# Four loads of an opening moved to later places in their queues: w_out's second half, two quarters of w_in, and the last slice of Bs

## The chip, the core and the metric

The kernel runs on one NeuronCore of a Trainium2 chip. A core has TensorE (PE, matmuls), VectorE (DVE), ScalarE (ACT), GpSimd (POOL) and SyncE (SP), each with its own instruction queue that is worked off in order, and 16 DMA engines that move data between the chip's memory (HBM) and the core's on-chip memory (SBUF). DMAs are issued by SP (here the profile's queue q1) and by POOL (q0); an issue is an instruction in that engine's queue. The metric is the device time of the whole kernel in microseconds (us). Before the change three runs gave 921.84, 922.67 and 922.73 us, median 922.67 us.

## The reference

Inputs are x (8 x 3008 x 256), two 256 x 256 matrices w_r and w_i with biases, and an expert layer w_in (256 x 2048) and w_out (2048 x 256), all float32.

```python
X = np.fft.rfft(x, axis=1)                        # per batch, along the 3008 positions
Yr = Xr @ w_r - Xi @ w_i + b_r
Yi = Xr @ w_i + Xi @ w_r + b_i
Y  = softshrink(Yr, 0.01) + 1j * softshrink(Yi, 0.01)
y  = np.fft.irfft(Y, n=3008, axis=1)              # back to 8 x 3008 x 256
h  = y.reshape(24064, 256) @ w_in
g  = np.where(h > 0, h, np.exp(np.minimum(h, 0)) - 1)      # ELU
out = g @ w_out                                   # 24064 x 256
```

## The kernel before

**Stages.** A batch's Fourier transform of length 3008 = 47 x 64 is done in stages of matmuls, with two passes through DRAM to reorder. For a batch b they are: A (six units: x times the 64-point table M1, written to DRAM as DA), Z (DA read back in another order, in two reads: slots 0 to 7, then slots 8 to 31), X (eight units on Z, giving XT), M (twelve units: XT times the weights, bias, softshrink, giving Y), B (six units on Y, written to DRAM as DB), Bs (DB read back in four slices, 0 to 3), and Y (eight units, two on each slice of Bs, giving yT). Then the expert layer takes yT in blocks of 512 tokens, and for each block in 8 steps: `front` (four matmuls of yT with w_in_s, and Exp), `elu` and `finish_elu` (DVE, sometimes POOL), and two steps later `back` (eight matmuls with w_out_r). Step i uses columns 256 (i mod 8) to 256 (i mod 8) + 255 of w_in: a quarter q of w_in, 512 columns, serves two steps, so quarter 2 is first used by front(4), quarter 3 by front(6). The second half of w_out is first used by back(4), which stands behind front(6).

**Order of the work.** Everything is written out by hand, and each engine's queue holds its instructions in the order of the program. An opening does all of batch 0 up to Bs, and stage A of batch 1, without expert work beside them. After it a loop over i runs the 376 steps of the expert layer, and a plan puts units of the next batches between its steps: f0[t] ahead of front(t), f1[t] behind `finish_elu`. For batch 0 the plan has Y(0,2) ahead of front(1), Y(0,3) to Y(0,5) ahead of front(2) to front(4), X(1,0) ahead of front(5), X(1,1) ahead of front(6), X(1,2) ahead of front(7), and Y(0,6), the first unit on slice 3 of Bs, ahead of front(21). In f1[3] a `gate` (a POOL copy of one column, which holds up POOL's queue until a tile has landed) waits for Z(1)'s second read, and then POOL issues the loads of x for batch 2 (in f1[3], f1[8] and f1[13]).

**Loads in the opening.** w_in comes in four quarters of 512 KB on SP's queue (`load_w_in`, L564), each into a staging tile, from where `scale_w_in` multiplies it by 2/S into the bf16 tile w_in_s (L641 on DVE for quarters 0 to 2, L643 on ACT for quarter 3). The order on SP's queue is: w_in(0); DB write 0; w_in(1); DB write 1; w_in(2); DB write 2; w_in(3); DB writes 3, 4, 5; Bs slices 0 and 1; DA write 0; Bs 2; DA write 1; Bs 3; DA write 2; the two reads of Z(1); then the output's writes. On POOL's queue: a gate on Z(0); the three loads of x for batch 1; w_out's two halves of 1 MB (`load_w_out`, L569); the softshrinks of `first_M` (L224, L225); the two halves of the table M4 (L632); the gate on Z(1) and the loads of x for batch 2; then the M units of batch 1 (L204, L205).

Between stages of the opening, `idle_pe(n)` (L292) puts n matmuls on a constant tile, whose result nobody reads.

Of the kernel before, what the change touches and what calls it, by code (L numbers as in the profile page):

```python
# [8 lines left out]
ALU = mybir.AluOpType  # L9
AF = mybir.ActivationFunctionType  # L10
# [19 lines left out]
def kernel(  # L30
# [11 lines left out]
    nc = tc.nc  # L42
    P = nc.NUM_PARTITIONS

    B, S, D = x.shape
# [59 lines left out]
    Bs_of = {}  # L105
# [22 lines left out]
    def unit_A(b, u, alone=False, on_dve=False, ahead=False):  # L128
        ci, uu = u // 2, u % 2
        if uu == 0:  # L130
            if ahead and ci > 0:
                A_of[b, ci] = late3.tile([P, 8, D], BF16, name="A", tag="gT")
            elif alone:
                A_of[b, ci] = wk4.tile([P, 8, D], BF16, name="A", tag="Bs")
            else:
                A_of[b, ci] = wk2.tile([P, 8, D], BF16, name="A", tag="A")
            if ci == 0:
                DA_of[b] = dram.tile([NJ, P, D], BF16, name="DA", tag="DA")
        xt, A = xts[ci], A_of[b, ci]
        dav = DA_of[b].rearrange("j p d -> p j d")  # L140
        ps = unit_ps("aps", alone or ahead)
        for j in range(2):
            nc.tensor.matmul(  # L143
                ps[:, j, :], lhsT=M1[:],
                rhs=xt[:, 4 * uu + 2 * j : 4 * uu + 2 * j + 2, :], start=True, stop=True,
            )
        evac(
            A[:, 4 * uu : 4 * uu + 4, :].rearrange("p n d -> p (n d)"),
            ps[:].rearrange("p a b -> p (a b)"), on_dve,
        )  # L150
        j0 = 8 * ci
        if alone:
            j0 += 4 * uu
            nc.sync.dma_start(dav[:, j0 : j0 + 4, :], A[:, 4 * uu : 4 * uu + 4, :])
        elif uu == 1:
            nc.sync.dma_start(dav[:, j0 : j0 + 8, :], A[:])

    def load_Z(b, s0, s1):

        if b not in Z_of:  # L160
            Z_of[b] = zp.tile([2 * NR, NS, D], BF16, name="Z", tag="Z")
        dv = DA_of[b].rearrange("j (h c s) d -> (j h c) s d", h=2, c=2)
        nc.sync.dma_start(Z_of[b][:, s0:s1, :], dv[:, s0:s1, :])
# [50 lines left out]
    def first_M(q, i, eng):  # L214

        ps = pre1.tile([P, 2 * D], F32, name="mps1", tag="mps1")
        yb, clip = m_group(0, q, i, ps[:])
        let_go()
        Y_ = Y_of[0, q][:, i, :]
        if eng is nc.scalar:  # L220
            nc.scalar.activation(clip[:], yb[:], AF.Relu, bias=lam_n[:])
            held.append((Y_, yb, clip))
        else:
            eng.tensor_scalar(clip[:], yb[:], LAM, -LAM, ALU.min, ALU.max)  # L224
            eng.tensor_tensor(Y_, yb[:], clip[:], ALU.subtract)  # L225
# [35 lines left out]
    def load_Bs(b, w):  # L261

        Bs = wk4.tile([4 * K1, 8, D], BF16, name="Bs", tag="Bs")
        dv = DB_of[b].rearrange("k (c h m) d -> (k c h) m d", c=2, h=2)
        nc.sync.dma_start(Bs[:], dv[:, 8 * w : 8 * w + 8, :])
        Bs_of[b, w] = Bs
# [22 lines left out]
    def idle_pe(n):  # L289

        for _ in range(n):
            nc.tensor.matmul(ips[:], lhsT=busy[:, 0:P], rhs=busy[:], start=True, stop=True)  # L292
# [264 lines left out]
    w_in_f = []  # L557

    def load_w_in(q):
        if q < 3:  # L560
            wf = late3.tile([P, 2, FQ], F32, name="w_in_f", tag="Et")
        else:
            wf = late2.tile([P, 2, FQ], F32, name="w_in_f", tag="osb")
        nc.sync.dma_start(wf[:], w_in_v[:, :, q * FQ : q * FQ + FQ])  # L564
        w_in_f.append(wf)

    def load_w_out(hh):
        hf = slice(hh * NFT // 2, (hh + 1) * NFT // 2)
        nc.gpsimd.dma_start(w_out_r[:, hf, :], w_out_v[:, hf, :])  # L569

    def gate(src):

        t = gatep.tile([P, 1], F32, name="gate", tag="gate")
        nc.gpsimd.tensor_copy(t[0 : src.shape[0], :], src)


    def fB(v, on_dve=False):
        unit_B(0, v, alone=True, on_dve=on_dve)
# [3 lines left out]
    for ci in range(3):  # L582
        load_x(1, ci)
    load_w_out(0)
    load_w_out(1)
    for u in range(8):
        unit_X(0, u, alone=True, on_dve=u in (1, 4, 7))
        if u == 1:
# [25 lines left out]
    first_M(2, 1, nc.scalar)  # L614
    first_M(3, 0, nc.gpsimd)
    fB(1)
    load_w_in(2)
    first_M(3, 1, nc.scalar)
    first_M(4, 0, nc.gpsimd)
    fB(2)  # L620
    load_w_in(3)
    first_M(4, 1, nc.scalar)
    first_M(5, 0, nc.scalar)
    fB(3)
# [6 lines left out]
    for h, w in enumerate((w40, w41)):  # L631
        nc.gpsimd.tensor_scalar(  # L632
            M4v[:, :, h], r4[0 : 2 * NR], w[0 : 2 * NR], None, ALU.mult
        )
    load_Bs(0, 0)
    load_Bs(0, 1)

    def scale_w_in(q, on_dve):
        dst = w_in_s[:, :, q * FQ : q * FQ + FQ]
        if on_dve:  # L640
            nc.vector.tensor_scalar_mul(dst, w_in_f[q][:], 2.0 / S)  # L641
        else:
            nc.scalar.activation(dst, w_in_f[q][:], AF.Copy, scale=2.0 / S)  # L643


    scale_w_in(0, True)
    for u in range(6):
        unit_A(1, u, on_dve=bool(u % 2), ahead=True)
        if u in (1, 3):
            scale_w_in((u + 1) // 2, True)  # L650
            load_Bs(0, 2 + u // 2)
        idle_pe(2)
    scale_w_in(3, False)
    for s0, s1 in ((0, 8), (8, NS)):
        load_Z(1, s0, s1)
    idle_pe(3)
    for u in range(2):
        unit_Y(0, u, alone=True, on_dve=bool(u % 2))
# [117 lines left out]
    def put(kind, b, *a):  # L776
        return ({"A": unit_A, "X": unit_X, "M": unit_M, "B": unit_B, "Y": unit_Y}[kind], (b, *a))

    def plan(b):

        f0 = [[] for _ in range(PER)]
        f1 = [[] for _ in range(PER)]
        n1, n2 = b + 1, b + 2
        mid = [("X", u) for u in range(8)] + [
            ("M", 0, 0), ("M", 0, 1), ("M", 1, 0), ("M", 1, 1), ("B", 0), ("M", 2, 0),
            ("M", 2, 1), ("B", 1), ("M", 3, 0), ("M", 3, 1), ("B", 2), ("M", 4, 0),
            ("M", 4, 1), ("B", 3), ("M", 5, 0), ("M", 5, 1), ("B", 4),
            ("A", 0), ("B", 5), ("A", 1), ("A", 2), ("A", 3), ("A", 4),
        ]
        if n1 < B:  # L790
            lead, seq = int(b == 0), [("y", u) for u in range(2, 6)] + mid
            seq.insert(20, ("y", 6))
            seq.insert(24, ("y", 7))
            xs = (3, 8, 13)
            seq += [("A", 5), ("n", 0), ("n", 1)] if b else [("n", 0), ("n", 1), ("A", 5)]
        else:
            lead, seq = 0, [("y", u) for u in range(2, 8)]
        for t, u in enumerate(seq, lead):
            if u[0] == "y":
                f0[t].append(put("Y", b, u[1]))  # L800
            elif u[0] == "n":
                f0[t].append(put("Y", n1, u[1]))
            elif u[0] == "A":
                if n2 < B:
                    f0[t].append(put("A", n2, u[1]))
            else:
                f0[t].append(put(u[0], n1, *u[1:]))
            if u == ("A", 1):
                f1[t] += [(load_Bs, (n1, w)) for w in range(4)]
            if u == ("A", 5) and n2 < B:  # L810
                f1[t] += [(load_Z, (n2, s0, s1)) for s0, s1 in ((0, 8), (8, NS))]
        if b == 0:
            f1[xs[0]].append((lambda: gate(Z_of[1][:, 16, 0:1]), ()))
        if n2 < B:
            for ci in range(3):
                f1[xs[ci]].append((load_x, (n2, ci)))
        return f0, f1
# [3 lines left out]
    for i in range(n + LAG):  # L821
        if i < n:
            r = i % PER
            if r == 0:
                f0, f1 = plan(i // PER)
                used = [bool(u0 or u1) for u0, u1 in zip(f0, f1)]
            free = not used[r]
            bare = bare + 1 if free else 0
            calm = free and (i >= n - 2 or (r + 2 < PER and not used[r + 1] and not used[r + 2]))
            for f, a in f0[r]:  # L830
                f(*a)
            on_act = any(f is unit_M for f, a in f0[r])
            h = front(i, calm and bare % 3 == 2, on_act)
        finish_elu()
        if i < n:
            for f, a in f1[r]:
                f(*a)
            split = not free and i > LAG and (i - LAG) % NPAIR == NPAIR - 1
            if split:
                back(i - LAG, True)  # L840
            elu(i, *h, free and i > 0, on_act)
        else:
            split = False
        if i >= LAG and not split:
            back(i - LAG, False)
# [30 lines left out]
```

## Time and profile before

| What | Value |
|---|---|
| median of three runs | 922.67 us |
| the profiled execution, its own time | 922.12 us |
| its span | 920.3 us |
| PE busy | 897.0 us, 97% of the span |
| DVE busy | 753.4 us, 82% |
| ACT busy | 695.0 us, 76% |
| POOL busy | 263.3 us, 29% |
| SP's queue (q1) | 77.61 MB |
| POOL's queue (q0) | 27.26 MB |

The profile's times are microseconds from the start of the span. A line of the timeline gives start, duration, engine, line of the kernel, operation, output and inputs, number of instructions and, in brackets, how long the engine sat idle before it and what ended that. SPq and POOL rows with DMA_DIRECT2D are the issues of transfers; the transfer itself runs later. "DMA Z<-DA" in the chain is the time from an issue to the landing of its last byte. PE's busy time includes the filler matmuls. The granted clock is 1.00 when TensorE runs at full speed.

### The profile page before, as it was taken

The page shows a single profiled execution, that of the slowest core. Times are in us where ns is not written, and L with a number is a line of the kernel's source. Part 1 is how long each engine was busy: PE and PEld are TensorE (multiplying, and loading weights), DVE is VectorE, ACT ScalarE, POOL GpSimd, SP SyncE. Part 2 cuts the span into 40 slices and gives each one's busy share as a digit, 9 for nine tenths or more (in the row PEclk, how much of TensorE's full clock was granted, in tenths as well). Part 3 has the DMA queues.
Part 4 walks back from the last instruction along what each step waited for, and adds up shares of the span by engine and source line. Part 5 has one row for each costly group of instructions (what it writes and reads, how often), then busy time and mean ns, then how long its engine had stood idle before and what let it go on. Part 6 is the DMA issues. An engine that isn't in the chain of part 4 may idle for free.

```text
span 920.3 us, 17019 instructions
## 1 busy us (share of the span) xinstructions
PE 897.0 (97%) x6711; PEld 648.5 (70%) x6711; DVE 753.4 (82%) x880; ACT 695.0 (76%) x767; POOL 263.3 (29%) x344
## 2 busy tenths in 40 slices
PE   8889999999999999999999999999999999999997
PEld 3347667776678676886678766787667867677775
DVE  8778778887788778887788877898778877798997
ACT  6667788777878778788786888778786878666664
POOL 6702430133311441205402153013331044211332
PEclk9999999999999999999999999999999999999999
DMA  8984216621283215723166031842137111421111
GB/s 267 354 255 146 88 47 187 204 69 47 81 229 126 70 47 150 195 92 92 53 200 184 24 107 55 226 142 87 52 96 204 41 30 47 114 57 36 34 37 46
DMA packets 90655, 106.21 MB, mean 115 GB/s; under 512 B 5264, under 2 KB 81296, under 8 KB 87216
## 3 DMA queue, kind: packets, MB, share of 16 engines
q1 hardware_dynamic: 84320, 77.61, 30.1%
q0 software_dynamic: 5968, 27.26, 9.1%
q8 instruction: 52, 0.85, 0.4%
q10 hardware_dynamic: 288, 0.26, 0.1%
q14 instruction: 27, 0.22, 0.1%
HBM read 55.31 MB, written 49.81 MB: 114 GB/s over the span
## 4 chain that ended last, share of the span: by engine, by line
PE 63%; DVE 21%; issue 5%; ACT 5%; DMA 4%; POOL 1%; DVEq 0%; SPq 0%; ACTq 0%; POOLq 0%
PE hps L695 24%; PE ps_o L752 23%; DVE gT L720 11%; PE mps L189 9%; DVE Et L731 4%; ACT Et L709 2%; PE bps L238 2%; DVE gT L722 2%; DVE Et L733 2%; PE xps L174 2%; PE aps L143 2%; PE yps L276 2%; DMA Z<-DA 1%; DMA DA<-A 1%; POOL Et L731 1%
## 5 line engine op out<-in xcount | busy, mean ns | idle before, releaser
L752 PE MATMUL ps_o<-w_out_r,gT 128*128 128x256 f32 x3008 | 473.0, 300 | 0.9 <-DVE gT L720 0.9
L752 PEld LDWEIGHTS ps_o<-w_out_r,gT 128*128 128x128 f32 x3008 | 399.2, 189 | 55.5 <-DVE gT L720 13.2
L695 PE MATMUL hps<-yT,w_in_s 128*128 128x512 bf16 (+7 forms) x1728 | 388.5, 352 | 6.7 <-DVE gT L720 2.5
L709 ACT ACTIVATE Et<-hps 128x1024 f32<-128x1024 f32 x291 | 299.8, 1030 | 84.5 <-PE hps L695 78.0
L720 DVE SCALAR_TENSOR_TENSOR gT<-Et,hps 128x1024 fp32r<-128x1024 f32 (+1 forms) x179 | 216.8, 1212 | 52.8 <-ACT Et L707 36.6
L722 DVE SCALAR_TENSOR_TENSOR gT<-hps,Et 128x1024 fp32r<-128x1024 f32 x198 | 242.0, 1222 | 16.3 <-DVE Et L733 0.5
L695 PEld LDWEIGHTS <-w_in_s 128*128 128x128 bf16 x1728 | 144.2, 98 | 137.3 <-issue 26.9
L733 DVE TENSOR_SCALAR Et<-Et 128x1024 f32<-128x1024 f32 x198 | 136.9, 691 | 45.3 <-ACT Et L709 37.9
L204 POOL TENSOR_SCALAR clip<-yb 128x512 f32<-128x512 f32 x84 | 51.7, 616 | 323.4 <-DVE yb L196 280.0
L706 ACT ACTIVATE Et<-hps 128x1024 f32<-128x1024 f32 x84 | 86.3, 1027 | 72.9 <-PE hps L695 72.4
L731 POOL TENSOR_SCALAR Et<-Et 128x512 f32<-128x512 f32 x94 | 59.8, 637 | 279.3 <-ACT Et L709 278.0
L205 POOL TENSOR_TENSOR Y<-yb,clip 128x512 bf16<-128x512 f32 x84 | 107.2, 1277 | 7.0
L196 DVE TENSOR_TENSOR yb<-mps,bias_bc 128x512 f32<-128x512 f32 x96 | 66.0, 689 | 36.6 <-PE mps L189 30.0
L707 ACT ACTIVATE Et<-Et 128x1024 f32<-128x1024 f32 x84 | 88.8, 1057 | 2.7
L126 ACT CAST XT<-xps 128x768 bf16<-128x768 f32 x61 | 48.7, 800 | 15.6 <-PE xps L174 15.6
L189 PE MATMUL mps<-wcat_r,XT 128*128 128x512 bf16 x192 | 58.8, 388 | 0.9 <-ACT XT L126 0.6
L126 ACT CAST yT<-yps 128x752 bf16<-128x752 f32 x63 | 49.7, 789 | 13.0 <-PE yps L276 12.9
L189 PE MATMUL mps<-wcat_s,XT 128*128 128x512 bf16 x192 | 57.7, 382 | 0.0
L126 ACT CAST A<-aps 128x1024 bf16<-128x1024 f32 x45 | 45.6, 1014 | 16.0 <-PE aps L143 14.4
L731 DVE TENSOR_SCALAR Et<-Et 128x512 f32<-128x512 f32 x94 | 54.1, 576 | 0.9 <-ACT Et L709 0.8
L189 PEld LDWEIGHTS <-XT 128*128 128x128 bf16 x384 | 30.7, 98 | 30.7 <-issue 2.5
L251 ACT CAST Bz<-bps 128x1024 bf16<-128x1024 f32 x46 | 46.0, 1000 | 2.9 <-PE bps L238 2.9
(102 smaller groups left out, 402.4 us busy)
## 6 DMA issues: line engine op xcount, KB each, us to landing
xt<-in_x_dram POOLq DMA_DIRECT2D x21, 1024.0 KB, 5.8
out_dram<-osb SPq DMA_DIRECT2D x158, 128.0 KB
Bs<-DB SPq DMA_DIRECT2D x32, 384.0 KB
DA<-A SPq DMA_DIRECT2D x21, 512.0 KB
DB<-Bz SPq DMA_DIRECT2D x21, 512.0 KB
Z<-DA SPq DMA_DIRECT2D x7, 1152.0 KB
Z<-DA SPq DMA_DIRECT2D x11, 384.0 KB
xt<-in_x_dram POOLq DMA_DIRECT2D x6, 512.0 KB, 6.2
```

The costliest lines, as they stand in the source:

```text
L126: nc.scalar.copy(dst, src)
L189: nc.tensor.matmul(ps, lhsT=XT[:, dt, c, o : o + P], rhs=wm[:, dt, :], start=(m == 0 and dt == 0), stop=(m == 1 and dt == 1),)
L205: nc.gpsimd.tensor_tensor(Y_of[b, q][:, i, :], yb[:], clip[:], ALU.subtract)
L695: nc.tensor.matmul(hps[:, s, c0:c1], lhsT=w_in_s[:, dt, ft * P : ft * P + P], rhs=yT_of[b][:, dt, t0 : t0 + c1 - c0], start=(dt == 0), sto ...
L706: nc.scalar.activation(E_, hps[:], AF.Relu, scale=-1.0)
L707: nc.scalar.activation(E_, E_, AF.Exp, scale=-1.0)
L709: nc.scalar.activation(E_, hps[:], AF.Exp)
L720: nc.vector.scalar_tensor_tensor(o, e, -1.0, h, ALU.add, ALU.max)
L722: nc.vector.scalar_tensor_tensor(o, h, 0.0, e, ALU.max, ALU.add)
L731: eng.tensor_scalar(E_[:, s], E_[:, s], 1.0, 0.0, ALU.min, ALU.max)
L733: nc.vector.tensor_scalar(E_, E_, 1.0, -1.0, ALU.min, ALU.add)
L752: nc.tensor.matmul(po[q][:, i_ % 2, :], lhsT=gT[:, s, i_ * P : i_ * P + P], rhs=w_out_r[:, ft, :], start=(ft == 0 and i_ % 2 == 0), stop=( ...
```

## The change

Four loads and the work that hangs on them change places; nothing is added to what is computed.

- w_out's second half goes on POOL's queue behind a new gate on slice 1 of Bs, which stands behind the two M4 instructions.
- w_in(2) goes on SP's queue behind DB write 5, ahead of Bs 0. Its scaling goes from DVE to ACT, to the place where quarter 3 was scaled.
- w_in(3) goes behind the two reads of Z(1). Its scaling goes from ACT to POOL, in f1[2], ahead of the gate on Z(1).
- Bs 3 goes behind w_in(3).

DB writes 2 to 5 thus follow each other on SP's queue with no load of w_in between them, and so do DA writes 1 and 2 with no Bs 3 between them.

```diff
     load_w_out(0)
-    load_w_out(1)
...
     fB(1)
-    load_w_in(2)
...
     fB(2)
-    load_w_in(3)
...
+    load_w_in(2)
     load_Bs(0, 0)
     load_Bs(0, 1)
-
-    def scale_w_in(q, on_dve):
+    gate(Bs_of[0, 1][:, 0, 0:1])
+    load_w_out(1)
+
+    def scale_w_in(q, eng):
         dst = w_in_s[:, :, q * FQ : q * FQ + FQ]
-        if on_dve:
-            nc.vector.tensor_scalar_mul(dst, w_in_f[q][:], 2.0 / S)
+        if eng is nc.scalar:
+            nc.scalar.activation(dst, w_in_f[q][:], AF.Copy, scale=2.0 / S)
         else:
-            nc.scalar.activation(dst, w_in_f[q][:], AF.Copy, scale=2.0 / S)
+            eng.tensor_scalar(dst, w_in_f[q][:], 2.0 / S, None, ALU.mult)
...
-    scale_w_in(0, True)
+    scale_w_in(0, nc.vector)
     for u in range(6):
         unit_A(1, u, on_dve=bool(u % 2), ahead=True)
-        if u in (1, 3):
-            scale_w_in((u + 1) // 2, True)
-            load_Bs(0, 2 + u // 2)
+        if u == 1:
+            scale_w_in(1, nc.vector)
+            load_Bs(0, 2)
         idle_pe(2)
-    scale_w_in(3, False)
+    scale_w_in(2, nc.scalar)
     for s0, s1 in ((0, 8), (8, NS)):
         load_Z(1, s0, s1)
+    load_w_in(3)
+    load_Bs(0, 3)
...
         if b == 0:
+            f1[2].append((scale_w_in, (3, nc.gpsimd)))
             f1[xs[0]].append((lambda: gate(Z_of[1][:, 16, 0:1]), ()))
```

## The prediction

> **What bounds the kernel now.** PE is busy for 897.0 of 920.3 us, so a loss or a gain has to be looked for where PE really waits. That is the opening, where the changed loads lie. I read the chain of waits first, for the transfers that lie on it.
>
> ```profile
> 50.06 2.26 DMA DB<-A
> ...
> 52.40 4.14 DMA Bs<-DB
> ...
> 57.78 6.99 DMA DA<-A
> ...
> 64.86 4.38 DMA Z<-DA
> ```
>
> The reader sees DB's last write, Bs 0, DA's last write and Z(1)'s first read, each issued when the one before has landed or its data is ready. Next the timeline of PE, for how late each of them is, and the first use of each load.
>
> ```profile
> 56.59 0.84 PE L276 MATMUL yps<-M,Bs 96*128 96x94 bf16 x16 [0.57 <-DMA Bs<-DB]
> ...
> 69.28 0.51 PE L174 MATMUL xps<-M,Z 96*128 96x96 bf16 x8 [0.34 <-DMA Z<-DA]
> 69.63 1.03 PE L695 MATMUL hps<-yT,w_in_s 128*128 128x512 bf16 x4
> ...
> 71.78 1.03 PE L695 MATMUL hps<-yT,w_in_s 128*128 128x512 bf16 x4
> ```
>
> PE waits 0.57 us for Bs 0 and 0.34 us for Z(1): these two are all that earlier landings can win. The row at 71.78 is the seventh of its kind (58.47, 59.67, 62.67, 64.83, 66.98, 69.63, 71.78), so it is front(6), the first user of w_in's quarter 3. Then POOL's timeline:
>
> ```profile
> 20.60 3.09 POOL L508 TENSOR_SCALAR wcat_s<-w_i_f 128x512 bf16<-128x512 f32 x1
> ...
> 73.29 0.18 POOL L574 CAST gate<-Z 96x1 f32<-96x1 bf16 x1 [26.84 <-DMA Z<-DA]
> 73.79 1.56 POOL L115 DMA_DIRECT2D xt<-in_x_dram  x2 [0.32 <-issue]
> ```
>
> The gate ends its wait when Z(1)'s second read has landed, so that is at 73.2. After the change w_in(3) is behind that read on the same queue, while its user stands at 71.78. That is the core of my forecast. Last, stretches of DMA share and of the granted clock (the last two columns but one are these), and what moved from 38.9 to 42:
>
> ```profile
> 52.00:53.30 1.30, 1.30 (x6) 0.75 (x6) 1.07 (x3) 0.78 (x1) 0.00 (x0) 1.00 0.00 0
> 64.10:66.00 1.90, 1.90 (x20) 1.47 (x19) 1.54 (x3) 1.55 (x3) 0.00 (x0) 1.00 0.11 25
> 33.40:36.82 3.42, 1.69 (x13) 0.80 (x13) 3.34 (x4) 1.29 (x3) 3.10 (x3) 1.00 1.08 403
> 36.82:40.23 3.41, 3.41 (x16) 1.05 (x14) 2.58 (x4) 2.09 (x4) 2.65 (x3) 0.50 1.82 358
> 60.71:64.12 3.41, 1.94 (x17) 1.45 (x17) 3.21 (x4) 2.53 (x4) 0.00 (x0) 1.00 0.99 314
> ```
>
> ```profile
> DMA packets 1063, 1.08 MB, mean 348 GB/s; under 512 B 16, under 2 KB 1062, under 8 KB 1062
> q0 software_dynamic: 1058, 1.07, 185.2%
> q1 hardware_dynamic: 4, 0.00, 0.5%
> ```
>
> The DMA engines stand empty at 52.0 to 53.3 and 64.1 to 66.0. A stretch in which PE worked 1.69 of 3.42 us is followed by one at half clock; one with 1.94 of 3.41 us is not.
>
> **The change part by part.** The sum is made against the profiled execution's own time, 922.12 us, which is 0.55 us under the median of 922.67; I carry the difference in time over to the median.
>
> *Before 50 us: nothing.* w_out's second half leaves POOL's queue at 27.43, where POOL then sat idle 2.42 us waiting for DVE's yb; the five softshrink pairs and the two M4 instructions behind it start no earlier. w_in(2) and w_in(3) leave SP's queue at 41.35 and 43.98 (0.51 us each), where SP then waits for ACT's Bz. DB's writes get an emptier path, but only the last counts, and it is bound by its data: issued at 50.06 when DVE had finished, landed 2.26 us later. Gain 0 to 0.2 us; I take 0.
>
> *w_in(2) ahead of Bs 0.* It is issued from 50.45, when the last DB write's issue is over; 0.52 MB at 348 GB/s is 1.5 us, of which the empty 1.3 us from 52.0 cover most. Bs 0 lands 0.2 us later (bounds: 0 and 1.5, the whole transfer). Behind it wait Bs 1, the three DA writes and Bs 2, equally. Its scaling on ACT takes the place that quarter 3's had (1.06 us at 54.72, ahead of 1.35 us of idle time), and DVE loses 0.68 us at 54.05 before a wait for PE: nothing.
>
> *Bs 3 away from DA write 2.* It was 0.39 MB on the queue ahead of that write, from 57 to 64 us at 332 GB/s on average: 1.2 us less. It is needed first at 107.76 us, so its later place costs nothing. DA's last write lands at 64.77 + 0.2 - 1.2 = 63.8 and Z(1) is issued at 63.9 instead of 64.86.
>
> *w_out's second half.* The gate copies (0.18 us) when Bs 1 has landed, soon after Bs 0's 56.54 plus its own 0.39 MB, about 57.9; after the 0.3 us before the next issue (the row at 73.79), the issue of 1.1 us ends near 59.5. The transfer is 1.05 MB at 348 GB/s, 3.0 us. Where do they fall? In the stretch from 38.9 to 42 the second half moved alone, with 4 packets on q1, although SP had issued a DB write at 37.88: what was issued first went first. DA write 2, whose data is ready at 56.2, is issued ahead of w_out, so w_out follows it, from 63.1 (before, the engines emptied at 64.1; less 1.0) to 66.1. Z(1)'s first data came 66.0 before; it now has to come behind w_out at 66.1. So Z(1) keeps its time, +0.1 us; bounds -1.0 (w_out hidden altogether) and +2.0 (all 3.0 us ahead of DA write 2). back(4), which needs it, is at 72.5: covered.
>
> The Trainium skill, in "DMA: Bandwidth & Descriptors", section "Queues, rings and completion order", states otherwise than the row from 38.9: each DMA engine takes turns between the queues, packet by packet. By it w_out would share the engines with DA writes 1 and 2 and Z(1) come up to 2.0 us late: the second rival's price, not needed for mine.
>
> *w_in(3) behind Z(1).* Z(1) lands at 73.2 + 0.1, and 1.5 us later (0.52 MB at 348 GB/s) w_in(3): 74.8. POOL is free for it: behind the gate and the issue of w_out, the scaling waits at the head of POOL's queue from 59.5. Behind it stand the gate on Z(1), the loads of x for batch 2 (used from 135.40) and the clip at 88.61, which had 13.26 us of idle time: nobody there is late.
>
> *The scaling on POOL.* 128 x 1024 float32 to bf16 is on no row. Two of the 128 x 512 TENSOR_SCALARs of L204 (0.616) make 1.2 us; two of L508 (3.09, also a multiply into bf16) make 6.2. During L508 DVE was busy until 22.33; at 74.8 DVE has nothing to do, because PE has stopped. I take 1.3 us, by the uncontended row, and keep 6.2.
>
> The Trainium skill, "SBUF — State Buffer", section "Who interferes with whom", has a reason for this choice: GpSimd and a DVE instruction with two SBUF inputs exclude each other. DVE ran such ones at 20.86 and 21.39, next to L508; by the page the copy here would be the short one.
>
> *The sum on PE.* front(6) starts at 74.8 + 0.1 + 1.3 = 76.2 instead of 71.78: +4.4 us. The 0.2 us at Bs 0 and whatever happens to X(1,0) lie inside this wait. PE stops for about 4.3 us, longer than a 3.41 us stretch, so the clock is halved as at 36.82. Depending on where the stretches fall, 1.8 to 5.2 us of work run at half clock, 3.4 on average; pairs of L189 matmuls took 1.06 instead of 0.59 us there, starts 0.86 instead of 0.43 apart. Half of 3.4 is 1.7 us (0.9 to 2.6). Nothing gives it back: from 76 us on PE is the bound, and its remaining waits follow from its own work. Total +6.1 us: 928.2 on the profiled execution's scale, **928.8 us** on the median's.
>
> **The rivals.**
>
> *w_out's packets go between those of DA.* All of it ahead of DA write 2 gives Z(1) +2.0 instead of +0.1: +8.0 us, 930.7. Against it speaks the stretch from 38.9; for it, that this was one case with a deep queue on the other side.
>
> *A slow copy on POOL.* 6.2 instead of 1.3: +11.0 us, 933.7. For it speaks L508; against it L507, a cast to bf16 of the same size, 0.61.
>
> *No stop at front(6): not slower.* If w_in(3), in larger packets of another source, is moved beside Z(1) and not behind it, it could land about 4 us after its issue at 64.9, at 69; with 1.3 us of copy, 70.3. The point that decides is a landing by 70.4. Then PE keeps its places, and wins at most 0.34 at Z(1) and loses 0.2 at Bs 0: 922.5, no change. Against it: DA write 2, issued at 57.78, took 6.99 us to land behind transfers of its own queue.
>
> **How the numbers follow.** The forecast has 0.58 (its own range 926.3 to 930.0, from the bounds of Z(1) down to -1.0 and of the clock), w_out between DA 0.20, the slow copy, in part or whole, 0.12, no stop 0.08; 0.02 for anything else. The range 926.0 to 933.0 leaves out the last two and the slow copy's upper half, 0.16. About 0.2%, 1.8 us, is what a measurement of this kernel tells from no change: only the no-stop case can end below 924.5. Faster 0.04, same 0.06, slower 0.90.
>
> **What would show it.** In the changed profile: a wait of 4 to 5 us of PE at L697 (front's line there) for POOL's scaling; that row at 74 to 75 us, 1.2 to 1.5 us long, after a wait for w_in_f; a stretch of 0.50 clock after it; Bs 0's wait near 0.8 us; X(1,0) at 69 to 69.5 (71 for the second rival). I am wrong if front(6) starts before 73, or if the waits later in the kernel shrink by what was lost here.

## The result, and the profile after

The change made the kernel slower: 1.0113 times the time before, interval 1.0097 to 1.0128, which is 10.4 us (9.0 to 11.8). A second measurement of the same kernel gave a median of 931.23 us (930.29 to 933.27) against 922.96, a ratio of 1.0094 (1.0074 to 1.0114), or 8.7 us. The forecast was 6.1 us more, 928.8, in a range of 926.0 to 933.0: the sign was right, both intervals lie above the size, and 922.67 + 10.4 = 933.1 lies just above the range. The first profiled execution of the changed kernel is left out, because TensorE ran at 0.75 of its clock in all of it (1126.54 us); the profile below is that of the second measurement, whose execution took 933.27 us, the longest of its four, with a span of 931.5 against 920.3 us before.

PE's busy time, from the page after:

```profile
PE 899.7 (97%) x6711; PEld 650.2 (70%) x6711; DVE 753.6 (81%) x879; ACT 694.8 (75%) x767; POOL 265.6 (29%) x346
...
L697 PE MATMUL hps<-yT,w_in_s 128*128 128x512 bf16 (+7 forms) x1728 | 389.4, 353 | 14.8 <-POOL w_in_s L643 8.3
```

PE is busy 2.7 us longer with the same 6711 matmuls, so some of them ran slower; and of the 14.8 us that front's matmuls waited in the whole kernel, 8.3 us are one wait for the scaling on POOL. PE's timeline after shows where (start, duration, row, idle time before it):

```profile
57.76 0.84 PE L276 MATMUL yps<-M,Bs 96*128 96x94 bf16 x16 [1.26 <-DMA Bs<-DB]
...
69.94 0.52 PE L174 MATMUL xps<-M,Z 96*128 96x96 bf16 x8
...
80.94 1.89 PE L697 MATMUL hps<-yT,w_in_s 128*128 128x512 bf16 x4 [8.34 <-POOL w_in_s L643]
```

Front(6) starts at 80.94 instead of 71.78. X(1,0), the row at 69.94, waits for nothing: Z(1)'s first read is not what is late. Bs 0's wait has grown from 0.57 to 1.26 us. The chain of waits after, from the same stretch of the opening as the lines shown of before (start, duration, what):

```profile
50.56 2.61 DMA DB<-A
...
53.68 4.95 DMA Bs<-DB
...
58.87 0.92 POOL w_out_r L569
59.78 18.28 issue
...
78.12 2.77 POOL w_in_s L643
...
80.94 1.89 PE hps L697 x4
```

Z(1) is no longer on it: it runs over Bs 1, the issue of w_out behind the new gate, and then 18.28 us in which POOL's queue stands at the scaling and the chain names nothing. The timelines say what it stands for, which is a landing. SP's rows after:

```profile
50.56 0.36 SPq L254 DMA_DIRECT2D DB<-A  x1
50.97 0.51 SPq L564 DMA_DIRECT2D w_in_f<-in_moe_w_in_dram  x1
53.30 0.80 SPq L265 DMA_DIRECT2D Bs<-DB  x2
...
64.96 0.79 SPq L163 DMA_DIRECT2D Z<-DA  x2
65.79 0.47 SPq L564 DMA_DIRECT2D w_in_f<-in_moe_w_in_dram  x1
66.30 0.47 SPq L265 DMA_DIRECT2D Bs<-DB  x1
```

and POOL's:

```profile
78.12 2.76 POOL L643 TENSOR_SCALAR w_in_s<-w_in_f 128x1024 bf16<-128x1024 f32 x1 [18.34 <-DMA w_in_f<-in_moe_w_in_dram]
```

w_in(3) leaves SP at 65.79 and has landed by 78.12, 13.16 us after Z(1)'s issue began; then the scaling takes 2.76 us. Stretches of the profile after (length, busy time of PE, PEld, DVE, ACT and POOL, granted clock, DMA share, GB/s):

```profile
71.57:74.99 3.42, 1.03 (x14) 0.85 (x13) 2.64 (x3) 1.61 (x2) 0.00 (x0) 1.00 1.01 229
74.99:78.40 3.41, 0.00 (x0) 0.00 (x0) 0.00 (x0) 0.00 (x0) 0.28 (x1) 0.50 0.43 102
78.40:81.81 3.41, 0.87 (x3) 0.32 (x4) 0.00 (x0) 0.00 (x0) 3.41 (x4) 0.50 0.00 0
81.81:85.23 3.42, 3.42 (x20) 2.86 (x19) 1.20 (x2) 1.03 (x1) 0.41 (x1) 0.50 0.89 285
85.23:88.64 3.41, 3.41 (x29) 2.63 (x28) 2.02 (x3) 2.94 (x4) 0.00 (x0) 1.00 0.83 329
```

The clock is halved from 74.99 to 85.23, so PE's first 4.3 us after the stop (80.94 to 85.23) run at half speed. From front(6) to the end of the span it is 931.5 - 80.94 = 850.56 us, against 920.3 - 71.78 = 848.52 before. So the 11.2 us between the two spans are 9.16 us in front(6)'s start, where the forecast had 4.4, and 2.04 us behind it, where it had 1.7.

### The profile page after: what moved, and what is told of

Its sections match the earlier page's. It is cut to its first block, busy times and chain, and to the rows that moved or that the text cites. A ratio compares the mean times of both kernels' runs of the same rounds, so it can differ in the third digit from the quotient of the medians.

```text
span 1124.7 us, 17020 instructions
## 1 busy us (share of the span) xinstructions
PE 1108.7 (99%) x6711; PEld 765.3 (68%) x6711; DVE 753.9 (67%) x879; ACT 707.3 (63%) x767; POOL 284.6 (25%) x346
## 4 chain that ended last, share of the span: by engine, by line
PE 96%; issue 2%; DMA 1%; DVE 1%; POOL 0%; ACT 0%; SPq 0%; POOLq 0%
PE ps_o L754 38%; PE hps L697 38%; PE mps L189 9%; PE bps L238 3%; PE xps L174 2%; PE aps L143 2%; PE yps L276 2%; PE ips L292 1%; DMA Bs<-DB 0%; DMA xt<-in_x_dram 0%; POOL w_in_s L643 0%; DMA DB<-A 0%; DVE M L600 0%; ACT XT L126 0%; DVE yb L196 0%
## 5 line engine op out<-in xcount | busy, mean ns | idle before, releaser
L754 PE MATMUL ps_o<-w_out_r,gT 128*128 128x256 f32 x3008 | 577.7, 344 | 0.0
L754 PEld LDWEIGHTS ps_o<-w_out_r,gT 128*128 128x128 f32 x3008 | 481.0, 211 | 81.9 <-issue 53.9
L697 PE MATMUL hps<-yT,w_in_s 128*128 128x512 bf16 (+7 forms) x1728 | 492.6, 425 | 6.6 <-POOL w_in_s L643 4.7
L697 PEld LDWEIGHTS <-w_in_s 128*128 128x128 bf16 x1728 | 163.3, 111 | 186.4 <-issue 143.4
L733 POOL TENSOR_SCALAR Et<-Et 128x512 f32<-128x512 f32 x94 | 79.4, 845 | 335.9 <-ACT Et L711 334.4
L204 POOL TENSOR_SCALAR clip<-yb 128x512 f32<-128x512 f32 x84 | 51.7, 615 | 442.8 <-DVE yb L196 442.8
L189 PE MATMUL mps<-wcat_s,XT 128*128 128x512 bf16 x192 | 71.6, 457 | 0.0
L189 PE MATMUL mps<-wcat_r,XT 128*128 128x512 bf16 x192 | 70.3, 457 | 0.4 <-ACT XT L126 0.4
L189 PEld LDWEIGHTS <-XT 128*128 128x128 bf16 x384 | 35.0, 110 | 40.4 <-issue 21.2
L733 DVE TENSOR_SCALAR Et<-Et 128x512 f32<-128x512 f32 x94 | 40.1, 427 | 12.7 <-ACT Et L711 4.0
```

The source lines that it names most:

```text
L189: nc.tensor.matmul(ps, lhsT=XT[:, dt, c, o : o + P], rhs=wm[:, dt, :], start=(m == 0 and dt == 0), stop=(m == 1 and dt == 1),)
L697: nc.tensor.matmul(hps[:, s, c0:c1], lhsT=w_in_s[:, dt, ft * P : ft * P + P], rhs=yT_of[b][:, dt, t0 : t0 + c1 - c0], start=(dt == 0), sto ...
L733: eng.tensor_scalar(E_[:, s], E_[:, s], 1.0, 0.0, ALU.min, ALU.max)
L754: nc.tensor.matmul(po[q][:, i_ % 2, :], lhsT=gT[:, s, i_ * P : i_ * P + P], rhs=w_out_r[:, ft, :], start=(ft == 0 and i_ % 2 == 0), stop=( ...
```

## The experiments

For each profiled execution three readings are used: when front(6) starts; the rest from there to the end of the span (848.5 us before); and the time from Z(1)'s first issue to the start of w_in(3)'s scaling, called the landing time of w_in(3). For the times themselves, each kernel has its ratio to runs of the kernel before that were made beside it, with a 95% interval.

### The changed kernel again

The edit is none.

> The changed kernel once more, for a profile at full clock. Theory (front(6) waits for w_in's quarter 3): about 932 to 933 us; PE waits 7 to 9 us ahead of front(6), because from the last DB write's issue to the end of the copy on POOL the disturbed profile shows 30.1 us, and 50.1 + 30.1 = 80.2 against 71.78; stretches of half clock behind it. Rival (the loss lies elsewhere, spread over the loop): a wait of no more than 4.5 us ahead of front(6), and the rest of the 10 us at later places.

Measured: 1.0094 (1.0074 to 1.0114), and the profile above, with a wait of 8.34 us at front(6).

### One part alone: w_in(3)

```diff
 (against before)
     fB(2)
-    load_w_in(3)
...
-    scale_w_in(3, False)
     for s0, s1 in ((0, 8), (8, NS)):
         load_Z(1, s0, s1)
+    load_w_in(3)
...
         if b == 0:
+            f1[2].append((pool_scale, (3,)))     # nc.gpsimd.tensor_scalar(..., 2.0 / S, None, ALU.mult)
```

> The kernel before, with w_in(3) alone behind Z(1) and its scaling on POOL; w_out, w_in(2) and Bs 3 at their old places. Theory: most of the loss comes back: Z(1) lands at 73.2, w_in(3) 1.5 to 2.3 us later, the copy takes 1.3 to 2.8 us, so front(6) starts at 76 to 78.3 instead of 71.8, plus 1 to 3.5 us of half clock: 928 to 932.5 us. Rival (w_out between DMAs is what costs): within 2 us of 922.7.

Measured: 929.82 us, 1.0077 (1.0055 to 1.0099). The rows of SP, POOL and PE in its timeline:

```profile
65.01 0.77 SPq L163 DMA_DIRECT2D Z<-DA  x2
...
75.88 2.77 POOL L647 TENSOR_SCALAR w_in_s<-w_in_f 128x1024 bf16<-128x1024 f32 x1 [28.95 <-DMA w_in_f<-in_moe_w_in_dram]
...
78.70 1.89 PE L698 MATMUL hps<-yT,w_in_s 128*128 128x512 bf16 x4 [6.31 <-POOL w_in_s L647]
```

This one move makes most of the loss, about 7 us. Its landing time is 10.87 us, 2.3 us shorter than with the whole change, though Z(1) is issued at the same time.

### All but that part

```diff
 (against the changed kernel)
     fB(2)
+    load_w_in(3)
...
+        if u == 3:
+            scale_w_in(2, nc.vector)
         idle_pe(2)
-    scale_w_in(2, nc.scalar)
+    scale_w_in(3, nc.scalar)
...
-    load_w_in(3)
     load_Bs(0, 3)
...
-            f1[2].append((scale_w_in, (3, nc.gpsimd)))
```

> The changed kernel with w_in(3) back at its place behind DB write 2, scaled on ACT, and w_in(2) scaled on DVE; w_out, w_in(2) and Bs 3 stay moved. Theory: no stop at front(6); X(1,0) waits for Z(1) by what w_out and w_in(2) delay it, 0 to 2 us: 922 to 925 us. Rival (w_out and w_in(2) cost most): 928 us or more.

Measured: 923.12 us, 1.0005 (0.9995 to 1.0014); front(6) at 71.52. The moves of w_out, w_in(2) and Bs 3 cost nothing that can be measured as long as w_in(3) is early. Rows of SP, PE and POOL:

```profile
64.30 0.79 SPq L163 DMA_DIRECT2D Z<-DA  x2
65.13 0.43 SPq L265 DMA_DIRECT2D Bs<-DB  x1
...
74.59 0.51 PE L174 MATMUL xps<-M,Z 96*128 96x96 bf16 x8 [1.12 <-DMA Z<-DA]
...
74.60 0.18 POOL L574 CAST gate<-Z 96x1 f32<-96x1 bf16 x1 [15.66 <-DMA Z<-DA]
```

With w_out ahead of it and Bs 3 behind it on the queue, Z(1)'s second read has landed by the gate's start, 74.60 - 64.30 = 10.3 us after the issue; before it was 73.29 - 64.86 = 8.4 us. X(1,2) waits 1.12 us for it.

### The half clock behind the stop

Filler matmuls ahead of front(6)'s own, into the tile that it then overwrites, keep PE busy through most of the stop. The same lines were put into the changed kernel (34 of them) and into the kernel with w_in(3) alone (24).

```diff
+        if i == 6:
+            for _ in range(34):        # 24 with w_in(3) alone
+                nc.tensor.matmul(
+                    hps[:, 0, :], lhsT=busy[:, 0:P], rhs=busy[:], start=True, stop=True
+                )
```

> The changed kernel with 34 filler matmuls (7.3 us at full clock) ahead of front(6), into the PSUM tile that front(6) then overwrites: the stop stays, but PE is busy in it. Theory (the wait and a loss of clock behind it add up): 1.5 to 4 us faster than the changed kernel, 929 to 931 us, and no stretch of half clock after 72 us. Rival (the clock costs nothing, the wait is all): the same time as the changed kernel within 1 us.

> The kernel with w_in(3) alone moved, and 24 filler matmuls (5.2 us) in its wait of 6.3 us ahead of front(6). Its profile had PE at half clock from 78.7 to 84.3, which is 2.8 us of lost work, and without fillers it took 929.8 us. Theory (the clock's loss is real and adds to the wait): 926.5 to 928 us. Rival (the fillers change nothing, as with the 34 of the first test): 929 to 930.5 us.

Measured: 931.87 us, 1.0097 (1.0080 to 1.0115), in the changed kernel, and 929.37 us, 1.0076 (1.0063 to 1.0089), with w_in(3) alone. By these times neither gained, as the rival had it. The rest from front(6) on was nevertheless 848.39 and 848.22 us, as before, with no half clock behind front(6); in these two executions front(6) itself started later, at 82.81 and 79.88, behind a later opening (Z(1)'s issue at 65.56 and 66.35) and, in the first, a landing time of 14.39 us. With the 24 fillers, moreover, four of the six runs spent 2.1 to 2.8 us of their time outside the span, against 1.7 to 1.8 us in the runs of the kernel without them; no run shows why. So the second pair was measured again, both kernels beside the same runs of the kernel before.

> w_in(3) alone moved, once more, beside its version with fillers on the same chip. Both theories: 929 to 930.5 us.

> The same with 24 filler matmuls in the wait. The profiles so far show 848.2 and 848.4 us from front(6) to the end with fillers and 849.8 to 851.6 without; the medians showed nothing. Theory (the half clock behind the stop costs 1 to 3 us, and the openings' own half-clock stretches, which fall differently in each execution, hid it): 1 to 2.5 us below the version without. Rival (what the fillers win is lost elsewhere): within 0.7 us of it.

Measured: w_in(3) alone 930.55 us, 1.0089 (1.0074 to 1.0104); with the fillers 928.30 us, 1.0061 (1.0049 to 1.0073): 2.25 us less. Stretches of the first, without the fillers:

```profile
73.51:76.92 3.41, 0.00 (x0) 0.00 (x0) 0.00 (x0) 0.00 (x0) 2.19 (x1) 0.50 0.02 9
76.92:80.33 3.41, 2.78 (x10) 1.86 (x11) 0.00 (x0) 0.85 (x1) 1.93 (x4) 0.50 0.41 96
```

and of the second, with them:

```profile
74.00:77.40 3.40, 2.00 (x10) 0.69 (x7) 0.00 (x0) 0.00 (x0) 2.43 (x1) 1.00 0.01 2
77.40:80.80 3.40, 2.95 (x24) 2.23 (x25) 0.77 (x2) 1.68 (x2) 1.69 (x4) 1.00 0.47 120
```

PE does the same front(6) at 77.55 and 77.80 in these two executions, at half clock in the first and at full clock in the second. The half clock is real and its price can be read from where it ends: half of the time that PE works under it, to about 0.5 us.

| Kernel | front(6) | half clock until | half of what lies between | rest, less 848.5 |
|---|---|---|---|---|
| changed kernel | 80.94 | 85.2 | 2.1 | 2.0 |
| w_in(3) alone | 78.70 | 84.3 | 2.8 | 3.1 |
| w_in(3) alone, again | 77.55 | 80.3 | 1.4 | 1.3 |
| w_in(3) and Bs 3 | 79.56 | 82.5 | 1.5 | 1.5 |
| Bs 3 by POOL | 78.43 | 84.2 | 2.9 | 2.8 |
| scaling on DVE | 79.06 | 84.8 | 2.9 | 2.4 |
| scaling in two steps on POOL | 81.11 | 84.2 | 1.6 | 2.0 |
| w_out in its old place | 80.43 | 85.4 | 2.5 | 2.4 |
| Bs 3 in its old place | 83.03 | 85.7 | 1.3 | 1.3 |
| three with fillers | 77.80 to 82.81 | none | 0 | -0.3 to 0 |

### The scaling: on DVE, and in two steps on POOL

```diff
 (against the changed kernel)
-            f1[2].append((scale_w_in, (3, nc.gpsimd)))
+            f1[5].append((scale_w_in, (3, nc.vector)))
```

> The changed kernel with quarter 3 scaled on DVE, behind gT of step 4, instead of on POOL. The copy takes 0.68 us on DVE and took 2.76 on POOL. Theory (copy and landing add up on the path to front(6)): front(6) 2.1 us sooner, 929 to 930.5 us against 931 to 932. Rival (POOL's copy is covered, PE waits for something else): no difference.

Measured: 931.38 us, 1.0091 (1.0078 to 1.0104). DVE's and PE's timeline:

```profile
78.31 0.69 DVE L643 TENSOR_SCALAR w_in_s<-w_in_f 128x1024 bf16<-128x1024 f32 x1 [5.93 <-DMA w_in_f<-in_moe_w_in_dram]
...
79.06 1.89 PE L697 MATMUL hps<-yT,w_in_s 128*128 128x512 bf16 x4 [3.97 <-DVE w_in_s L643]
```

The scaling is 2.1 us shorter and front(6) starts 1.9 us sooner than in the changed kernel, but the median does not tell the two apart. In this execution the half clock lasted until 84.8: a stop that ends sooner leaves more work under the last stretch of half clock (the table above).

```diff
 (against the changed kernel)
+        elif eng is nc.gpsimd:
+            eng.tensor_scalar(w_in_f[q][:], w_in_f[q][:], 2.0 / S, None, ALU.mult)
+            eng.tensor_copy(dst, w_in_f[q][:])
```

> The changed kernel with POOL's multiply done in float32 in place, and then a plain copy to bf16, two instructions instead of one. If POOL is slow only where a multiply writes bf16 (2.76 us for 1024 columns): 1.2 us each, by L204 (0.616 for 512) and L507 (0.607 for 512), 2.4 in all. If it is slow by the two-row shape of the operands: each 2 us or more. Total within 1 us of the changed kernel either way.

Measured, in two runs only: 934.31 us, 1.0127 (1.0107 to 1.0147), 3 us above the changed kernel's 931.23 where at most 1 us was expected. POOL's timeline:

```profile
77.19 2.76 POOL L643 TENSOR_SCALAR w_in_f<-w_in_f 128x1024 f32<-128x1024 f32 x1 [18.25 <-DMA w_in_f<-in_moe_w_in_dram]
80.02 1.04 POOL L644 CAST w_in_s<-w_in_f 128x1024 bf16<-128x1024 f32 x1
```

A multiply on POOL takes 2.76 us with a float32 result too, and a cast of the same shape to bf16 takes 1.04. Neither the conversion nor the size is what makes it slow; the expectation's other case, slow by the shape of the operands, falls too, because the cast has the same shape.

### Where Bs 3 and w_out lie

Bs 3 back in its old place, ahead of DA write 2:

```diff
 (against the changed kernel)
+        if u == 3:
+            load_Bs(0, 3)
         idle_pe(2)
...
     load_w_in(3)
-    load_Bs(0, 3)
```

> The changed kernel with Bs 3 back ahead of DA write 2; w_out stays behind Bs 1, w_in(3) behind Z(1). If Bs 3 behind w_in(3) on the queue is what slows w_in(3) (landed 78.0, and 75.8 with w_in(3) alone moved), it lands 1 to 2 us sooner after Z(1)'s issue, while Z(1) itself comes 1.2 us later: total within 1 us of the changed kernel. If w_out's move is what slows it, w_in(3) still lands 13 us after Z(1)'s issue and the total is 1 us above the changed kernel's.

Measured: 933.27 us, 1.0115 (1.0100 to 1.0129), the rows of SP, POOL and PE:

```profile
57.12 2.86 SPq L265 DMA_DIRECT2D Bs<-DB  x1
60.07 0.44 SPq L156 DMA_DIRECT2D DA<-A  x1
70.08 0.77 SPq L163 DMA_DIRECT2D Z<-DA  x2
...
60.10 0.97 POOL L569 DMA_DIRECT2D w_out_r<-in_moe_w_out_dram  x1
...
74.25 0.51 PE L174 MATMUL xps<-M,Z 96*128 96x96 bf16 x8 [2.99 <-DMA Z<-DA]
```

The landing time falls to 10.12 us, but Bs 3's issue occupies SP for 2.86 us, DA write 2 is issued together with w_out, at 60.07, and lands only when Z(1) is issued, at 70.08. X(1,0) now waits 2.99 us. The queues' packets (number, MB, share of the 16 engines) show what each order of issue made of w_out, first in the changed kernel from 64.5 to 66.0 us,

```profile
q0 software_dynamic: 534, 0.54, 148.3%
q1 hardware_dynamic: 3, 0.01, 8.4%
```

then here from 65 to 69 us:

```profile
q0 software_dynamic: 984, 1.00, 95.8%
q1 hardware_dynamic: 466, 0.23, 27.5%
```

In the changed kernel w_out's first packet moved at 62.79, DA write 2's last one ended at 64.46, and from there w_out moved nearly alone until Z(1)'s first packet at 65.91, and beside Z(1) to its end at 66.90. Here the two moved side by side, w_out from 64.51 to 69.42 and DA write 2 until 69.47.

w_out's second half back in its old place:

```diff
 (against the changed kernel)
     load_w_out(0)
+    load_w_out(1)
...
-    gate(Bs_of[0, 1][:, 0, 0:1])
-    load_w_out(1)
```

> The changed kernel with w_out's second half back at its place behind the first. If w_out's move delays Z(1): Z(1) is issued near 64 and its second read lands near 72 to 73, w_in(3) at 74.5 to 76, front(6) at 77.3 to 79, total 928 to 930.5 us. If not: the same 931 to 932 us as the changed kernel.

Measured: 932.51 us, 1.0098 (1.0084 to 1.0113). The time is that of the changed kernel, and not the 928 to 930.5 us of the expectation's first case. The landing time fell to 11.96 us, but the opening was late in its execution: Bs 0 was issued at 54.37 instead of 53.30, and three stretches of half clock lay before 62 us, one in the changed kernel.

Bs 3 on POOL, behind the second load of x for batch 2:

```diff
 (against the changed kernel)
     load_w_in(3)
-    load_Bs(0, 3)
...
                 f1[xs[ci]].append((load_x, (n2, ci)))
+                if b == 0 and ci == 1:
+                    f1[xs[ci]].append((load_Bs, (0, 3, nc.gpsimd)))
```

> The changed kernel with Bs 3 neither behind w_in(3) nor ahead of DA write 2: POOL issues it behind the second load of x for batch 2. From the first issue of Z(1) to the landing of w_in(3) it took 13.1 us in the changed kernel and 10.3 to 11.1 with w_in(3) alone moved. If Bs 3 behind it slows it: 11 to 12 us here, and 1 to 1.5 us less in all. If w_out ahead of Z(1) is the whole of it: 13 us again and no change.

And w_in(3) alone with only Bs 3 behind it:

```diff
 (against w_in(3) alone)
-            load_Bs(0, 2 + u // 2)      # slices 2 and 3
+            load_Bs(0, 2)               # at u == 1
...
     load_w_in(3)
+    load_Bs(0, 3)
```

> w_in(3) and Bs 3 alone moved behind Z(1), w_out and w_in(2) at their old places. If Bs 3 behind it slows w_in(3): 11.5 to 12 us from Z(1)'s issue to its landing; Z(1) is issued 1.2 us sooner than with w_in(3) alone, so that front(6) and the total stay within 1 us of that kernel's 930 us. If not: 10.3 to 11.1 us, and 1 us less in all.

Measured: Bs 3 on POOL 931.59 us, 1.0097 (1.0080 to 1.0114), w_in(3) landing after 11.28 us, as expected, and the time no less, as not expected; w_in(3) with Bs 3 929.22 us, 1.0075 (1.0058 to 1.0093), landing after 12.08 us. The scalings in their POOL timelines, first Bs 3 on POOL,

```profile
75.61 2.76 POOL L643 TENSOR_SCALAR w_in_s<-w_in_f 128x1024 bf16<-128x1024 f32 x1 [16.20 <-DMA w_in_f<-in_moe_w_in_dram]
```

then w_in(3) with Bs 3, whose Z(1) is issued at 64.65:

```profile
76.73 2.77 POOL L647 TENSOR_SCALAR w_in_s<-w_in_f 128x1024 bf16<-128x1024 f32 x1 [28.93 <-DMA w_in_f<-in_moe_w_in_dram]
```

All executions together, sorted by what lies around w_in(3):

| | Bs 3 not behind w_in(3) | Bs 3 behind it |
|---|---|---|
| w_out early | landing time 10.35 to 11.15 (four executions), mean 10.8 | 11.96 and 12.08 |
| w_out between Bs 1 and Z(1) | 11.28 (Bs 3 on POOL); 10.12 with Z(1) issued at 70.08 (Bs 3 in its old place) | 13.09 to 14.39 (four) |

And from Bs 0's issue to Z(1)'s, the stretch in which DA's writes land: 11.8 to 12.5 us with Bs 3 among the DA writes and w_out early (five executions, mean 12.3); 10.8 to 11.3 with neither there (three, mean 11.0); 11.1 to 12.0 with w_out there (six, mean 11.6); 15.96 with both.

Which of the two transfers is late, Z(1)'s second read or w_in(3) behind it, shows where POOL's gate on Z(1) does not stand behind the scaling, as with the scaling on DVE:

```profile
65.22 0.79 SPq L163 DMA_DIRECT2D Z<-DA  x2
...
77.22 0.18 POOL L574 CAST gate<-Z 96x1 f32<-96x1 bf16 x1 [17.19 <-DMA Z<-DA]
```

Z(1)'s second read has landed only by 77.22, 12.0 us after the issue, and w_in(3), by 78.31, 1.1 us later. In the traces of the other runs the two can be told apart by the size of their packets: Z(1)'s second read is 96 of 12,288 bytes, w_in(3) 256 of 2,048. The end of the last packet of each, in fifteen executions:

| | Z(1)'s last packet, after Z(1)'s issue | w_in(3)'s last packet, after Z(1)'s |
|---|---|---|
| w_out not moving at Z(1)'s issue, Bs 3 not behind w_in(3) | 7.9 to 9.0 us (seven, two of them with w_in(3) early) | 1.4 to 1.6 us (five) |
| w_out not moving at Z(1)'s issue, Bs 3 behind | 7.8 and 8.1 | 3.5 and 3.3 |
| w_out still moving, Bs 3 not behind w_in(3) | 9.4 and 9.7 (the second with w_in(3) early) | 1.3 (one) |
| w_out still moving, Bs 3 behind | 9.6 to 12.0 (four) | 1.5 to 2.3 |

So two things add to the landing: w_out, where it still moves when Z(1) is issued (its last packet ended 1.6 to 4.6 us after the issue in the six executions of the lower rows), makes Z(1) late, and Bs 3 makes w_in(3) late. Where the edit is w_out alone, the changed kernel against the one with w_out back in its old place, Z(1)'s last packet came after 9.64 and 8.07 us. In all fifteen the middle one of Z(1)'s packets ended 5.2 to 6.2 us after the issue: it is the last packets that come late. Why those lag is not shown.

### Is there something better than the kernel before?

The one gain in the above is Bs 3 away from DA write 2. It was put into the kernel before, on POOL's queue as above, with a few fillers more where the opening drops to half clock.

```diff
 (against before)
-        idle_pe(34)
+        idle_pe(38)
...
+    idle_pe(6)
     fB(0)
...
-            load_Bs(0, 2 + u // 2)
+        if u == 1:
+            load_Bs(0, 2)
...
+    idle_pe(4)
     first.close()
...
+                if b == 0 and ci == 1:
+                    f1[xs[ci]].append((load_Bs, (0, 3, nc.gpsimd)))
```

> The kernel before, not the changed one, with Bs 3 issued by POOL behind the second load of x for batch 2 (needed at 107 us), and fillers where PE idles in the opening: 4 more ahead of X(0,0), 6 ahead of the first B unit, 4 behind Y(0,1). Theory (half clock in the opening costs 1.4 us for each stretch that falls there, and Bs 3 holds DA write 2 up by 1.2 us, of which PE feels 0.3): 920.8 to 922 us, 0.5 to 1.8 us faster than before. Rival (neither is on the path): within 0.5 us of before.

Measured: 921.97 us, 0.9998 (0.9989 to 1.0006): no difference. The gate on Z(1)'s second read started at 73.00, against 73.29 before, and the whole of what PE waited for Z(1) before was 0.34 us.

## Why the prediction was right in kind and short in size

**Right: the place and the mechanism.** PE stops at front(6) for w_in's quarter 3 and for nothing else; that move alone makes most of the loss, and without it nothing is left (1.0005). The stop is followed by half clock, and nothing later gives the time back: without half clock the rest is 848.2 to 848.5 us, as before. So the no-stop rival falls.

**Right: Bs 3 away from DA write 2, 1.2 us.** It measured 12.28 - 11.05 = 1.2 us from Bs 0's issue to Z(1)'s.

**Right in the order, short in the price: w_out behind DA write 2.** In the changed kernel w_out's packets moved mostly behind DA write 2's, so the rule of the Trainium skill ("DMA: Bandwidth & Descriptors", "Queues, rings and completion order") did not decide this case. But the order needs DA write 2 to be issued first. Where both were issued within 0.03 us of each other (Bs 3 back in place), they moved side by side, which agrees with the page's turns, and Z(1) was issued 3.7 us later than with Bs 3 there and w_out early (15.96 against 12.3 behind Bs 0's issue), the second rival's effect at nearly twice its 2.0 us. The forecast had w_out cost nothing ahead of Z(1)'s issue and 1.1 us behind it. It cost 11.6 - 11.0 = 0.6 us ahead, and behind it Z(1)'s last packet ended after 9.4 to 12.0 us (six executions, mean 10.4) instead of 7.8 to 9.0 (nine, mean 8.4).

**Wrong: the landing of w_in(3).** This is the step that failed, and the price of the scaling behind it. The forecast's landing time was 74.9 - 63.9 = 11.0 us, the execution's 13.16. Its first part was "Z(1) keeps its time": a landing at 73.3, 9.4 us after the issue. The last packet ended after 9.64 us, and a landing is felt about 0.5 us behind the last packet (72.80 and 73.29 before), so that Z(1) was some 0.7 us late. The second part was "1.5 us later w_in(3)". That holds where Bs 3 is not behind it (1.3 to 1.6 us in six executions); here Bs 3 was, and it was 2.3 us. So "its later place costs nothing" was wrong: I had looked only at when Bs 3 itself is needed, and not at whom it delays. Last, the scaling started 1.24 us behind w_in(3)'s last packet and not 0.5; that was so in no other execution (0.5 to 0.8) and stays unexplained. Together 0.7 + 0.8 + 0.7 = 2.2 us. The forecast priced each transfer by its size over the mean rate of 348 GB/s, but a landing waits for the last packets, and these came later than the mean rate says.

**Wrong: "the scaling on POOL, 1.3 us".** It took 2.76. L204, the row that was taken, is a maximum and a minimum; L508 is a multiply as this one. But neither row had the price: they made 1.2 and 6.2 us. Half of 2.76 is 1.38 us for 512 columns, 1.7 less than L508's 3.09; the two DVE instructions beside L508, at 20.86 and 21.39, took 0.60 and 0.94 us, which would about fill that difference if POOL stood still for them, but no run tests it. The reason that I drew from the Trainium skill ("SBUF — State Buffer", "Who interferes with whom") does not explain the 2.76 us: DVE did nothing from 74.99 to 81.81 (0.00 in both stretches) while the multiply ran. The slow-copy rival was right that the multiply is slow, but at 2.76 us and not at its 6.2.

**Smaller: the opening, and a sum.** DB's last write was issued 0.5 us later in this execution, and w_in(2) behind it made Bs 0's issue 2.74 instead of 2.34 us later than the write, so 0.4 instead of 0.2. Bs 0's wait was 1.26 instead of the 0.8 foretold. The forecast's own range does not follow from its bounds: Z(1) 1.1 us sooner and the clock at 0.9 to 2.6 make 926.9 to 929.7 and not 926.3 to 930.0; the measurement lies above both.

**The sum mended.** Opening 0.5, w_in(2) 0.2 more, Bs 0 to Z(1) 0.4 more (11.66 instead of 11.3), landing 2.2 more, scaling 1.5 more: about 4.7 us on top of the forecast's 4.4 makes the measured 9.16. The clock, 2.0 us, was inside its bounds of 0.9 to 2.6; over all executions it went from 1.3 to 3.1.

**What stays open.** The times do not show the terms one by one. Without Bs 3 behind w_in(3), or with the short scaling on DVE, front(6) started 1.9 to 2.5 us sooner in the profiled execution (Bs 3 on POOL, 78.43; scaling on DVE, 79.06), and the medians stayed at 931.6 and 931.4. One cause is shown: the end of the half clock does not move along with the stop, which took back 0.4 to 0.8 us (the rest of 2.4 and 2.8 against 2.0). Others are likely: the profiled execution of the changed kernel was the longest of its four (933.27 against 930.29 to 931.81), and the opening varies, with Z(1) issued at 66.35 and 63.82 in two executions of one kernel (w_in(3) alone with fillers). So the split holds for the 11.2 us between the profiled spans, and of the 8.7 to 10.4 us between the times only w_in(3)'s share of about 7 to 8 us and the nothing without w_in(3) are shown, and the fillers' 2.25 us for the one pair that was measured side by side.

## What to carry to other kernels

Before a load is moved to a later place, find the start of its first user in the timeline and add up the whole way there: the transfers ahead of it, those right behind it, and the conversion on the engine that it is given to. Price a transfer that others wait for by its last packets, not by its mean rate. Price an instruction by a row of the same operation on the same engine, and look at what ran beside that row: here another operation's row made 1.2 us, the same operation's 6.2, and it took 2.76. Where PE stops for longer than a stretch of the clock, add half of the work that the last stretch of half clock will cover, and expect a shorter stop to win less than its length.

## What the runs showed of the hardware that was not expected

- A multiply by a constant on POOL took 2.76 us for 128 x 1024 float32, with a bf16 and with a float32 result, against 1.04 us for a cast of that shape on POOL, and 0.69 us for the same multiply on DVE.
- A transfer lands with its last packets: Z(1)'s last one ended 7.8 to 9.0 us after the issue, and 9.4 to 12.0 us where w_out still moved at the issue, while the middle one of its packets moved only between 5.2 and 6.2 us.
- A transfer lands later when another is queued behind it: w_in(3)'s last packet came 1.3 to 1.6 us behind Z(1)'s without Bs 3's 0.39 MB behind it, and 3.3 and 3.5 us with it where w_out was early.
- Which transfer moves first went by the order of issue where one was issued well ahead (w_out nearly alone from 64.5 to 66.0 us, behind DA write 2), and both moved side by side where they were issued within 0.03 us.
- An issue on SP can be held up for long: Bs 3's took 2.33 us before and 2.86 with Bs 3 back in place, against 0.47 us behind w_in(3), and with that DA write 2 was no longer issued ahead of w_out.
- A stretch of 3.41 us with 1.03 us of PE's work was followed by half clock, one with 2.00 us was not; the stretches of the kernels begin at different times (74.99 and 73.51 above; 74.00 is reckoned from a later change of the clock), so the price of the same stop differs between executions.
